# Scores and values of an attention tile placed on TensorE part by part instead of as one chain, and tile 1's loads issued by ScalarE

## The chip, the cores and the metric

The kernel runs on one core of one Trainium2 chip. The metric is the time of one execution on the device in microseconds (us), the lower the better. A core has TensorE (PE, matrix products; its weight loads are listed as PEld), VectorE (DVE), ScalarE (ACT), GpSimd (POOL) and SyncE (SP), which issues most of the DMA transfers. The engines work beside one another and wait for one another through semaphores.

## What is computed

Attention over a window of 128 keys (4 batches, 8 heads, 576 positions, 64 values per head), then a token mixer and two channel MLPs:

```python
scores = q @ k.T / sqrt(64)
scores = where((rel >= 0) & (rel < 128), scores - slope * abs(rel), -1e9)   # rel = query - key
attn = softmax(scores)
x = attn @ v                                   # 4 x 576 x 512
h = relu(x.T @ w_tok1) @ w_tok2                # token mixer
u = x + h.T
x = u + relu(u @ w_ch1) @ w_ch2                # channel MLP, 512 -> 1536 -> 512
out = x + relu(norm(x) * g @ w_ch1b) @ w_ch2b  # second MLP, 512 -> 2048 -> 512
```

## The kernel before

The 2304 positions are cut into 18 tiles of 128. The program first lists operations, each with its engine, a cost, what it reads and what it writes; a planner (`Plan.order`) then plays the engines against these costs, and the order in which it starts the operations is the order in which the instructions are written, engine by engine. On the chip each engine works through its own list in that order. Among the operations that are ready the planner takes the one with the earliest due time, and the due times are worked out from the summed PE costs. The dictionary `pl.chain` makes it place one operation directly behind another; a chained operation must be ready as soon as its forerunner is.

In the attention stage a tile i goes through these steps:

- Scores (line 636): `packed(i, i2)` makes two parts, one for each of two PSUM banks `ps_s` (c = 0, 1). A part is 4 matmuls that use 64 rows of the array each, two at a time on its two halves; a tile that starts a batch (0 and 9) has 128 columns in a matmul, the others 256. The trace lists two instructions for a matmul on f32 here, so a part is 8 rows of the trace and both are 16.
- `softmax(i, c)`: VectorE copies part of the keys over (682), takes scores and bias together with a minimum (688), ScalarE takes the exponentials (697), PE transposes four 128x128 blocks into the one PSUM bank `ps_t` (704), ScalarE (for the first tiles also VectorE) copies them to `pf` (377, 383), and GpSimd masks them (715).
- Values (648): two parts again, 8 matmuls each (4 for a tile that starts a batch), each using 64 columns of the array, two at a time. `normalize` copies them to `ut`, transposes them back (727) and scales them into `u` (393).

In the kernel before, `packed` puts the two scores parts of tile i + 1 and the two values parts of tile i - 1 into one chain on PE. Its first operation is given all that the others read and write (`also`), so that the chain starts only when both banks and both `pf` are there. The costs have 200 ns added at its first and its last operation.

Between these, PE does the token mixer (472 to 474 and 788 to 790: three matmuls of 512 columns for a product, called a triple here), whose weights VectorE, ScalarE and GpSimd convert from 64-bit numbers on the way (441 on ScalarE; 444, 446, 448, 456 on VectorE; one set of these per weight block). After the attention the channel MLPs follow (1177 to 1179 and 1312 to 1314).

The loads: SyncE issues tile 0's keys and queries in halves (568), then tile 1's keys and queries (572 and 369), tile 2's and so on. ScalarE issues the bias (847) and then loads its table (850).

Of the kernel before, what the change touches and what calls it, by code (L numbers as in the profile page):

```python
# [24 lines left out]
P = 128  # L25
DM = H * D
# [5 lines left out]
WINDOW = 128  # L32
RING = 4
WT2_PARTS, FIRST_TILES = 3, 3
CT = 4
CW = CT * P
HW = CW // 2
# [76 lines left out]
class Plan:  # L114
# [22 lines left out]
    def buf(self, pool, shape, dtype, tag, bufs=1):  # L137
        b = Buf(self, pool, shape, dtype, tag, bufs)
        ring = self.rings.setdefault((pool, tag), [])
        if len(ring) >= bufs:  # L140
            b.after = [ring[-bufs]]
        if ring:
            b.behind = ring[-1]
        ring.append(b)
        return b
# [155 lines left out]
    def emit(self):  # L301
        for k in self.order():
            self.ops[k][1](self.taken[k])


def dve(n, fast=False):
    return 150 + n / (1.92 if fast else 0.97)
# [14 lines left out]
def pe(n):  # L322
    return 2.6 + n / 2.4
# [6 lines left out]
def block_kernel(tc, qT, kT, v, wt1, wt2, wa1, wa2, wb1, wb2, g, bias, out):  # L330
    nc = tc.nc
# [4 lines left out]
    def op(cost, emit, reads=(), writes=(), behind=()):  # L336
        return pl.op(cost, (lambda e: emit()) if len(cost) == 1 else emit, reads, writes, behind)
# [30 lines left out]
    def load(dst, get, nbytes, src):  # L368
        op({"DMA": max(nbytes / 360, 500)}, lambda: nc.sync.dma_start(out=get(), in_=src), writes=[dst])
# [124 lines left out]
    src = {"a1": wa1, "a2": wa2, "b1": wb1, "b2": wb2}  # L494
# [55 lines left out]
    bias_sb = buf("att", [P, 4, H, P], BF16, "bias_sb")  # L550
# [5 lines left out]
    keys = buf("att", [P, RING, H // 2, P], F32, "keys")  # L556
# [1 line left out]
    wt2h, wt2l = few()  # L558
    vs, qs = {}, {}

    def load_qk(i):
        r = i % RING
        b = qs[i] = buf("att", [P, H // 2, P], F32, "q", Q_BUFS)
        if i == 0:
            for c in range(2):
                def halves(h=slice(2 * c, 2 * c + 2)):
                    for x, src in ((keys.t[:, 0, h], kT), (b.t[:, h], qT)):
                        nc.sync.dma_start(out=x, in_=src[0].rearrange("p (h t) -> p h t", t=P)[:, h])

                op({"DMA": 1000 if c == 0 else P * DM * 4 / 360}, halves, writes=[b if c else (keys, 0)])  # L570
            return
        op({"DMA": 1000}, lambda: nc.sync.dma_start(out=keys.t[:, r].rearrange("p h t -> p (h t)"), in_=kT[i]),
           writes=[(keys, r)])
        load(b, lambda: b.t.rearrange("p h t -> p (h t)"), P * DM * 4, qT[i])

    def load_v(i):
        b = vs[i] = buf("atb", [P, H, D], F32, "v", 3)
# [25 lines left out]
    def keys_of(i):  # L603

        s = i % RING
        if starts_batch(i):
            return [i], 0, 0, (s, s + 1, 1)
        table = 3 if len(batches_of(i)) > 1 else 2 if len(batches_of(i - 1)) > 1 else 1
        if s == 0:
            return [i, i - 1], 0, table, (0, RING, RING - 1)  # L610
        return [i - 1, i], 1, table, (s - 1, s + 1, 1)
# [6 lines left out]
    def packed(i, i2):  # L618

        parts, ready = [], []
        if i is not None:
            tiles, own, table, (a0, a1, a2) = keys_of(i)
            w = len(tiles) * P
            x = qs[i]
            for c in range(2):
                ps_t[i, c] = buf("psa", [P, 2, 2, 2 * P], F32, "ps_s", 2)  # L630

                def scores(c=c, ps=ps_t[i, c]):
                    for p in range(2):
                        for j in range(2):
                            r = slice(j * D, (j + 1) * D)
                            nc.tensor.matmul(ps.t[:, j, p, :w], x.t[r, 2 * c + p], keys.t[r, a0:a1:a2, 2 * c + p],  # L636
                                             start=True, stop=True)

                parts.append((4 * pe(2 * w), scores, [x] + [(keys, t % RING) for t in tiles], [ps_t[i, c]]))
        if i2 is not None:  # L640
            tiles2 = keys_of(i2)[0]
            na = len(tiles2)
            for c in range(2):
                def values(c=c, pf=pf_t[i2, c]):
                    for p in range(2):
                        for a, kt in enumerate((i2, i2 - 1)[:na]):
                            for j in range(2):
                                nc.tensor.matmul(pv.t[j * D:(j + 1) * D, 2 * c + p], vs[kt].t[:, 4 * c + 2 * p + j],  # L648
                                                 pf.t[:, a, 2 * p + j], start=(a == 0), stop=(a == na - 1))

                parts.append((na * 440, values, [(pf_t[i2, c], a) for a in range(na)] + [vs[kt] for kt in tiles2],
                              [(pv, c)]))

        before = None
        for k, (cost, emit, reads, writes) in enumerate(parts):
            also = parts[k + 1:] if k == 0 else []
            now = op({"PE": cost + (200 if k in (0, len(parts) - 1) else 0)}, emit,
               reads + [x for p in also for x in p[2]], writes + [x for p in also for x in p[3]])
            if before is not None:
                pl.chain[before] = now  # L660
            before = now
        fill(before, 4 if i == 0 else 0)
# [7 lines left out]
    def fill(k, n):  # L670
        if n:
            pl.chain[k] = op({"PE": 0}, lambda: spin(n), [ident], [busy], [k])
# [127 lines left out]
    def attention():  # L800
# [16 lines left out]
        def bias_time(a, b, emit=lambda: None):  # L817
            return op({"DMA": (b - a) * P * P * H * 2 / 360}, emit, [], [(bias_sb, j) for j in range(a, b)])

        def make_bias():  # L820
# [15 lines left out]
            for c in range(2):  # L836
# [7 lines left out]
               one, [(bias_sb, 3)])  # L844

        load_qk(0)
        first = bias_time(0, 1, lambda: nc.scalar.dma_start(out=bias_sb.t[:, 1, 0], in_=bias))
        warm = buf("small", [P, 1], F32, "warm")
        op({"DVE": 60}, lambda: nc.vector.memset(warm.t, 0.0), [], [warm])
        op({"ACT": 1400}, lambda: nc.scalar.activation(out=warm.t, in_=warm.t, func=AF.Exp), [], [warm], [first])  # L850
        load_qk(1)
        make_bias()
        bias_time(1, 2)
        op({"DVE": 0}, lambda: None, [(bias_sb, 0), (bias_sb, 1)], [(bias_sb, 1)])
        load_v(0)
        load_v(1)
        load_qk(2)
        tok_later = []

# [6 lines left out]
        for i in range(-1, NTILE + 1):  # L866
# [15 lines left out]
            for c in range(2):  # L882
# [4 lines left out]
                m, r = divmod(n - WT_START, WT_STEP)  # L887
# [53 lines left out]
    def prep_wide(layer, tiles):  # L941
# [10 lines left out]
        def quadrant(r, c, kk):  # L952
            return turned(layer, [(tiles[CT * c + t], 2 * r + kk) for t in range(CT)])

# [117 lines left out]
    def fast2(s):  # L1072
        layer, c, _, n = steps[s]
        return (layer, c) in FAST2 and n < (NF1, NF2)[layer] // 2 - 1
# [218 lines left out]
    def second(s, w2, hid):  # L1293

        layer, _, tiles, n = steps[s]
        turns = list(enumerate(tiles))
        if s == len(steps) - 1:
            turns = turns[CT:] + turns[:CT]
        for t, i in turns:
            if len(tiles) == 2:  # L1300
                hs = [(*hid[0], j, j * HW + t * P) for j in range(2)]
            else:
                hs = [(*hid[j, t // CT], None, t % CT * P) for j in range(2)]
            if s == len(steps) - 1 and t == turns[-1][0]:
                last_tile(w2, hs, i)
                yield
                continue
            o = buf("pst", [P, DM], F32, "tok", 2)

            def emit(o=o, hs=hs):  # L1310
                for j, ((wh, wl), (hh, hl, _, c)) in enumerate(zip(w2, hs)):
                    nc.tensor.matmul(o.t, hh.t[:, c:c + P], wh.t, start=j == 0, stop=False)  # L1312
                    nc.tensor.matmul(o.t, hh.t[:, c:c + P], wl.t, start=False, stop=False)  # L1313
                    nc.tensor.matmul(o.t, hl.t[:, c:c + P], wh.t, start=False, stop=j == 1)  # L1314

            op({"PE": 6 * pe(DM)}, emit, [x for w in w2 for x in w] + [(x, key) for hh, hl, key, _ in hs for x in (hh, hl)], [o])
            op({"DVE": dve(DM)}, lambda o=o, i=i: nc.vector.tensor_tensor(u[i].t, o.t, u[i].t, ALU.add), [o], [u[i]])  # L1317
            if layer == 1 and n == NF2 // 2 - 1:
                op({"DMA": 728}, lambda i=i: nc.sync.dma_start(out=out[i * P:(i + 1) * P, :], in_=u[i].t), [u[i]])
            yield  # L1320

    def second_fast(s, w2, hid):
# [8 lines left out]
        for g in range(2):  # L1331
            first, other = tiles[2 * g], tiles[CT + 2 * g]
            groups.append([first, other, g, {}])
# [124 lines left out]
    w1, pieces, before = begun(), None, None  # L1458
    load_w(used[0] + W_BUFS)
    for s in range(len(steps) + 1):  # L1460
# [7 lines left out]
        if len(tiles) == 2:  # L1468
            parts, ns = two_blocks(w1, xs, hid), (4, 4)
        else:  # L1470
            parts = seven_products(w1, xs, keep, s == len(steps) - 1, hid, fast2(s))
# [41 lines left out]
        before = s, w2, hid  # L1513
# [41 lines left out]
```

## Time and profile before

| | before |
|---|---|
| time, median of 3 runs | 832.47 us (832.24 to 832.49) |
| the profiled execution, its own time | 832.61 us |
| its span, first to last instruction | 830.9 us |
| PE busy | 820.7 us (99%) |
| DVE busy | 660.7 us (80%) |
| POOL busy | 471.7 us (57%) |
| ACT busy | 429.5 us (52%) |

A span is cut into stretches by the view of windows, which gives the busy time of each engine in each stretch. A busy PE is not a PE at its pace: a matmul's shown duration covers its way through the array, and the next one starts before it ends. What PE needs for a piece of work is therefore read from the starts of successive instructions, not from their durations. Idle time that the views show in front of an instruction is shorter than the time lost there, for the same reason.

### The profile page before, as it was taken

The numbers are of one execution on the slowest core, as the hardware profiler recorded it, in microseconds if no ns is written. First come the engines' busy times: TensorE is split into PE (matmuls) and PEld (weight loads), VectorE is DVE, ScalarE is ACT, GpSimd is POOL, SyncE is SP. The second block draws the span as 40 slices with busy tenths as digits, with TensorE's granted clock in tenths as the row PEclk, the third lists the DMA queues.
The fourth block names the chain that finished last, engine by engine and source line by source line (L and its number), as shares of the span: only waits on it lengthen the run. The fifth ranks groups of instructions, "written<-read, shape, count | busy, mean of one in ns | idle before, by whom it ended". The sixth has DMA issues, their size and how long they took to land.

```text
span 830.9 us, 14390 instructions
## 1 busy us (share of the span) xinstructions
PE 820.7 (99%) x4743; PEld 692.4 (83%) x4743; DVE 660.7 (80%) x1384; ACT 429.5 (52%) x1017; POOL 471.7 (57%) x728
## 2 busy tenths in 40 slices
PE   8999999999999999999999999999999999999998
PEld 6777788888888898888888888888889889999997
DVE  6889777969788979987879868989666767777785
ACT  7888777643344544334368333437456634444440
POOL 4785456746354567534248666857543556666650
PEclk9999999999999999999999999999999999999999
DMA  8578745545668889987862544888977663443302
GB/s 310 170 197 292 240 148 175 167 159 178 219 223 288 294 316 320 350 282 248 284 219 65 183 156 143 289 311 292 348 265 240 228 224 130 133 145 118 102 26 101
DMA packets 80618, 178.19 MB, mean 214 GB/s; under 512 B 9248, under 2 KB 11680, under 8 KB 80544
## 3 DMA queue, kind: packets, MB, share of 16 engines
q1 hardware_dynamic: 79920, 175.94, 62.5%
q0 software_dynamic: 480, 1.31, 0.7%
q8 instruction: 37, 0.61, 0.3%
q14 instruction: 37, 0.30, 0.1%
q10 hardware_dynamic: 144, 0.03, 0.0%
HBM read 137.14 MB, written 38.80 MB: 212 GB/s over the span
## 4 chain that ended last, share of the span: by engine, by line
PE 92%; DVE 4%; ACT 2%; issue 1%; POOL 0%; DVEq 0%; ACTq 0%
PE b L1177 10%; PE tok L1312 10%; PE tok L1314 10%; PE b L1178 10%; PE tok L1313 10%; PE b L1179 10%; PE tok L1349 5%; PE p L1349 4%; PE ps_s L636 3%; PE ps_v L648 3%; PE p L930 2%; PE b L474 2%; PE b L473 2%; PE b L472 2%; PE ps_t L704 1%; ACT pr L697 1%
## 5 line engine op out<-in xcount | busy, mean ns | idle before, releaser
L1317 DVE TENSOR_TENSOR u<-tok,u 128x512 f32<-128x512 f32 x195 | 133.7, 687 | 52.7 <-PE tok L1314 51.3
L1312 PE MATMUL tok<-w2h,hh 128*128 128x512 f32 x390 | 153.3, 393 | 0.0
L1314 PE MATMUL tok<-w2h,hl 128*128 128x512 f32 x390 | 152.1, 390 | 0.1
L1313 PE MATMUL tok<-w2l,hh 128*128 128x512 f32 x390 | 152.2, 390 | 0.0
L1177 PE MATMUL b<-xh,w1h 128*128 128x512 f32 x384 | 150.4, 392 | 0.3 <-DVE b L393 0.3
L1178 PE MATMUL b<-xl,w1h 128*128 128x512 f32 x384 | 149.8, 390 | 0.0
L1179 PE MATMUL b<-xh,w1l 128*128 128x512 f32 x384 | 149.6, 389 | 0.0
L395 POOL TENSOR_TENSOR w1l<-w,w1h 128x256 fp32r<-128x256 f32 (+1 forms) x112 | 79.4, 730 | 111.1 <-ACT w1h L377 97.0
L1008 ACT ACTIVATE hh<-b 128x512 fp32r<-128x512 f32 (+1 forms) x112 | 58.6, 541 | 140.6 <-PE b L1179 99.9
L1314 PEld LDWEIGHTS tok<-w2h,hl 128*128 128x128 f32 x390 | 73.2, 188 | 16.4 <-DVE hl L1010 0.8
L1312 PEld LDWEIGHTS tok<-w2h,hh 128*128 128x128 f32 x390 | 73.3, 188 | 15.0 <-DVE u L1317 0.8
L1010 DVE SCALAR_TENSOR_TENSOR hl<-b,hh 128x512 fp32r<-128x512 f32 (+1 forms) x112 | 67.2, 617 | 23.0 <-ACT hh L1008 22.5
L1313 PEld LDWEIGHTS tok<-w2l,hh 128*128 128x128 f32 x390 | 73.3, 188 | 14.2
L1179 PEld LDWEIGHTS b<-xh,w1l 128*128 128x128 f32 x384 | 72.1, 188 | 15.4
L1177 PEld LDWEIGHTS b<-xh,w1h 128*128 128x128 f32 x384 | 72.2, 188 | 14.5 <-DVE b L393 0.7
L1178 PEld LDWEIGHTS b<-xl,w1h 128*128 128x128 f32 x384 | 72.2, 188 | 13.5
L395 POOL TENSOR_TENSOR w1l<-st,w1h 128x256 fp32r<-128x256 f32 x58 | 44.9, 796 | 48.6 <-ACT w1h L377 42.7
L441 ACT ACTIVATE e<-rh 128x512 bf16<-128x512 bf16 (+2 forms) x62 | 39.7, 640 | 62.5 <-DMA rh<-wb 30.3
L697 ACT ACTIVATE pr<-t,mn 128x128 f32<-128x128 f32 x144 | 55.9, 391 | 10.1 <-DVE mn L688 10.0
L715 POOL TENSOR_SCALAR_AFFINE_SELECT pf<-pf 128x512 f32<-128x512 f32 x64 | 42.2, 660 | 33.3 <-ACT pf L377 26.3
L393 DVE TENSOR_TENSOR b<-b,p 128x512 f32<-128x512 f32 x56 | 38.9, 695 | 20.0 <-PE b L1179 19.5
L395 POOL TENSOR_TENSOR xl<-st,xh 128x256 fp32r<-128x256 f32 x48 | 39.0, 834 | 21.0 <-ACT xh L377 16.6
(215 smaller groups left out, 1931.2 us busy)
## 6 DMA issues: line engine op xcount, KB each, us to landing
w<-d SPq DMA_DIRECT2D x86, 256.0 KB, 4.3
rw<-wb SPq DMA_DIRECT2D x32, 512.0 KB, 5.2
rh<-wb SPq DMA_DIRECT2D x32, 512.0 KB, 5.0
rw<-wa SPq DMA_DIRECT2D x24, 512.0 KB, 4.3
rh<-wa SPq DMA_DIRECT2D x24, 512.0 KB, 4.5
d<-y SPq DMA_DIRECT2D x30, 256.0 KB, 5.4
v<-v SPq DMA_DIRECT2D x18, 256.0 KB, 3.8
keys<-kT SPq DMA_DIRECT2D x17, 256.0 KB, 4.5
```

The lines of the kernel that those rows point to most:

```text
L395: ENGINE[e].tensor_tensor(get()[:, c], ga()[:, c], gb()[:, c], alu)
L697: op({"ACT": 580}, lambda m=m: nc.scalar.activation(out=pr.t[:, m], in_=t.t[:, m], func=AF.Exp, bias=mn.t[:, m:m + 1], scale=-1.0, accum_o ...
L1008: op({"ACT": act(n, True)}, lambda: nc.scalar.activation(out=hh.t[:, c], in_=go(), func=AF.Relu), [o], [(hh, key)])
L1010: mark[0] = op({"DVE": dve(n)}, lambda: nc.vector.scalar_tensor_tensor(out=hl.t[:, c], in0=go(), scalar=0.0, in1=hh.t[:, c].bitcast(F32), ...
L1177: nc.tensor.matmul(g.t, wh.t[:, w], xh.t, start=start and k == 0, stop=False, skip_group_check=True)
L1178: nc.tensor.matmul(g.t, wh.t[:, w], xl.t, start=False, stop=False, skip_group_check=True)
L1179: nc.tensor.matmul(g.t, wl.t[:, w], xh.t, start=False, stop=stop and k == 1, skip_group_check=True)
L1312: nc.tensor.matmul(o.t, hh.t[:, c:c + P], wh.t, start=j == 0, stop=False)
L1313: nc.tensor.matmul(o.t, hh.t[:, c:c + P], wl.t, start=False, stop=False)
L1314: nc.tensor.matmul(o.t, hl.t[:, c:c + P], wh.t, start=False, stop=j == 1)
L1317: op({"DVE": dve(DM)}, lambda o=o, i=i: nc.vector.tensor_tensor(u[i].t, o.t, u[i].t, ALU.add), [o], [u[i]])
L1349: nc.tensor.matmul(o.t[:, p], x()[:, c], y(), start=start and p == 0 and k == 0, stop=stop and p == 1 and k == 2, skip_group_check=True)
```

## The change

- A table `SPLIT` names all 18 tiles. For these the parts are no longer chained, the first no longer takes over what the others read and write, and each part's cost has 100 ns added, instead of 200 at the first and the last.
- Tile 1's keys and queries are issued by ScalarE, right behind the bias and ahead of its table load, and no longer by SyncE. The two operations in the planner stay, with nothing to issue.

```diff
+SPLIT = range(18)
...
-    def load_qk(i):
+    def load_qk(i, ahead=None):
...
-        op({"DMA": 1000}, lambda: nc.sync.dma_start(out=keys.t[:, r].rearrange("p h t -> p (h t)"), in_=kT[i]),
-           writes=[(keys, r)])
-        load(b, lambda: b.t.rearrange("p h t -> p (h t)"), P * DM * 4, qT[i])
+        def start(k, queue=nc.sync):
+            x, src = ((lambda: keys.t[:, r], kT), (lambda: b.t, qT))[k]
+            queue.dma_start(out=x().rearrange("p h t -> p (h t)"), in_=src[i])
+
+        for k, x in enumerate(((keys, r), b)):
+            op({"DMA": (1000, P * DM * 4 / 360)[k]}, (lambda: None) if ahead else (lambda k=k: start(k)), writes=[x])
+        return lambda: [start(k, ahead) for k in range(2)]
...
-            also = parts[k + 1:] if k == 0 else []
-            now = op({"PE": cost + (200 if k in (0, len(parts) - 1) else 0)}, emit,
+            also = parts[k + 1:] if k == 0 and i not in SPLIT else []
+            now = op({"PE": cost + (100 if i in SPLIT else 200 if k in (0, len(parts) - 1) else 0)}, emit,
                reads + [x for p in also for x in p[2]], writes + [x for p in also for x in p[3]])
-            if before is not None:
+            if before is not None and i not in SPLIT:
                 pl.chain[before] = now
...
-        first = bias_time(0, 1, lambda: nc.scalar.dma_start(out=bias_sb.t[:, 1, 0], in_=bias))
+        first = bias_time(0, 1, lambda: (nc.scalar.dma_start(out=bias_sb.t[:, 1, 0], in_=bias), second()))
...
-        load_qk(1)
+        second = load_qk(1, nc.scalar)
```

The last chains have no scores in them (i is None), and stay as they were. In the changed kernel the lines stand 5 further down (scores 641, values 653, transposes 709 and 732; the lines ahead of `load_qk` 1 further: the triples 473 to 475, the weight conversion 445, 447, 449 and 457).

On PE, early in the attention stage (tiles 5 to 7). Before:

```order
L636 MATMUL ps_s<-keys,q 128x256 x8
L648 MATMUL ps_v<-pf,v 64x128 x16
L704 MATMUL ps_t<-ident,pr 128x128 x4
L727 MATMUL ps_v<-ident,ut 128x128 x4
L472 MATMUL tok<-xh,wt1h_406 128x512
L473 MATMUL tok<-xl,wt1h_406 128x512
L474 MATMUL tok<-xh,wt1l_423 128x512
L704 MATMUL ps_t<-ident,pr 128x128 x4
L472 MATMUL tok<-xh,wt1h_406 128x512
```

Now:

```order
L641 MATMUL ps_s<-keys,q 128x256 x4
L709 MATMUL ps_t<-ident,pr 128x128 x4
L653 MATMUL ps_v<-pf,v 64x128 x16
L641 MATMUL ps_s<-keys,q 128x256 x4
L709 MATMUL ps_t<-ident,pr 128x128 x4
L732 MATMUL ps_v<-ident,ut 128x128 x4
L641 MATMUL ps_s<-keys,q 128x256 x4
L709 MATMUL ps_t<-ident,pr 128x128 x4
L653 MATMUL ps_v<-pf,v 64x128 x16
```

The two scores parts of a tile stand apart, each alone between transposes and values, and the triples that stood between the transposes are gone from this place and come later.

On VectorE, at the same tiles (`t` is the scores with their bias, `mn` their minimum, `s`, `m` and `y` a weight block on its way). Before:

```order
L732 RECIPROCAL rc<-rc 128x8
L393 TENSOR_TENSOR u<-ps_v,rc 128x512
L444 TENSOR_SCALAR s<-e 128x128
L446 SCALAR_TENSOR_TENSOR s<-e,s 128x128
L456 SCALAR_TENSOR_TENSOR y<-m,s 128x256
L448 TENSOR_SCALAR m<-rw 128x256
L682 COPY_PREDICATED ps_s<-after,ps_s 128x4x128 x2
L688 ISA t,mn<-ps_s,bias_sb 128x128
```

Now:

```order
L693 ISA t,mn<-ps_s,bias_sb 128x128
L693 ISA mn 128x1
L445 TENSOR_SCALAR s<-e 128x96
L449 TENSOR_SCALAR m<-rw 128x192
L447 SCALAR_TENSOR_TENSOR s<-e,s 128x96
L687 COPY_PREDICATED ps_s<-after,ps_s 128x4x128
L457 SCALAR_TENSOR_TENSOR y<-m,s 128x192
L693 ISA t,mn<-ps_s,bias_sb 128x128
```

Before, the scores of both banks come together, with one weight block for a tile; now they come bank by bank, and a weight block stands between the banks as well.

On PE, late in the attention stage (the scores of tile 16). Before:

```order
L704 MATMUL ps_t<-ident,pr 128x128 x4
L636 MATMUL ps_s<-keys,q 128x256 x8
L648 MATMUL ps_v<-pf,v 64x128 x16
L472 MATMUL tok<-xh,wt1h_406 128x512
L473 MATMUL tok<-xl,wt1h_406 128x512
```

Now:

```order
L795 MATMUL tok<-hh,fewl 128x512
L641 MATMUL ps_s<-keys,q 128x256 x4
L709 MATMUL ps_t<-ident,pr 128x128 x4
L653 MATMUL ps_v<-pf,v 64x128 x16
L641 MATMUL ps_s<-keys,q 128x256 x4
L709 MATMUL ps_t<-ident,pr 128x128 x4
```

Where PE went from its whole array to scores, to values and back once, it now goes to scores, back, to values, to scores and back.

## Rows read from the trace of the kernel before

**Rows 1.** Windows: busy us (x instructions) per engine, granted clock, DMA share, GB/s.

```profile
6.03:50.70 44.67, 42.28 (x404) 33.12 (x401) 37.80 (x177) 36.62 (x145) 27.20 (x49) 1.00 0.71 234
...
48.47:88.05 39.58, 37.16 (x360) 29.31 (x358) 34.68 (x152) 33.53 (x127) 25.98 (x51) 1.00 0.83 260
88.05:156.56 68.51, 68.51 (x548) 56.52 (x548) 54.91 (x164) 47.23 (x142) 40.93 (x60) 1.00 0.58 192
156.56:830.90 674.34, 670.01 (x3446) 571.83 (x3444) 534.51 (x905) 310.61 (x607) 375.08 (x558) 1.00 0.63 213
```

**Rows 2.** Timeline of PE around one chain: start us, us, engine, line, operation.

```profile
96.37 2.00 PE L636 MATMUL ps_s<-keys,q 64*128 64x256 f32 x16
98.29 1.97 PE L648 MATMUL ps_v<-pf,v 128*64 128x128 f32 x32
100.19 0.66 PE L704 MATMUL ps_t<-ident,pr 128*128 128x128 f32 x4
...
102.08 0.60 PE L727 MATMUL ps_v<-ident,ut 128*128 128x128 f32 x4
102.51 0.60 PE L704 MATMUL ps_t<-ident,pr 128*128 128x128 f32 x4
```

**Rows 3.** Timeline of PE in four narrow windows inside that chain.

```profile
96.90 0.60 PE L636 MATMUL ps_s<-keys,q 64*128 64x256 f32 x4
...
97.77 0.60 PE L636 MATMUL ps_s<-keys,q 64*128 64x256 f32 x4
...
98.78 0.50 PE L648 MATMUL ps_v<-pf,v 128*64 128x128 f32 x6
...
99.77 0.50 PE L648 MATMUL ps_v<-pf,v 128*64 128x128 f32 x6
```

**Rows 4.** Timeline of PE around values that stand alone, late in the stage.

```profile
135.48 0.40 PE L473 MATMUL tok<-xl,wt1h 128*128 128x512 f32 x1
135.71 0.40 PE L474 MATMUL tok<-xh,wt1l 128*128 128x512 f32 x1
136.04 1.97 PE L648 MATMUL ps_v<-pf,v 128*64 128x128 f32 x32
137.93 0.50 PE L472 MATMUL tok<-xh,wt1h 128*128 128x512 f32 x1
138.28 0.40 PE L473 MATMUL tok<-xl,wt1h 128*128 128x512 f32 x1
```

**Rows 5.** Timeline of PE: tile 1's scores, with the idle time ahead of them.

```profile
7.59 2.00 PE L636 MATMUL ps_s<-keys,q 64*128 64x256 f32 x16 [0.61 <-DVE mn L688]
```

**Rows 6.** PE's groups by form from 48.47 to 88.05 us: busy, mean ns | idle, releaser.

```profile
L648 PE MATMUL ps_v<-pf,v 128*64 128x128 f32 x176 | 10.9, 276 | 0.0
L704 PE MATMUL ps_t<-ident,pr 128*128 128x128 f32 x48 | 8.7, 289 | 1.7 <-ACT pf L377 1.5
L636 PE MATMUL ps_s<-keys,q 64*128 64x256 f32 x66 | 8.4, 389 | 0.0
L727 PE MATMUL ps_v<-ident,ut 128*128 128x128 f32 x24 | 3.7, 276 | 0.3 <-ACT ut L377 0.3
L788 PE MATMUL tok<-hh,fewh 128*128 128x512 f32 x8 | 3.6, 448 | 0.0
...
L473 PE MATMUL tok<-xl,wt1h 128*128 128x512 f32 x2 | 0.9, 445 | 0.4 <-POOL xl L395 0.4
```

**Rows 7.** VectorE's groups from the start to 50.7 us, by line.

```profile
L688 DVE CUSTOM_DVE_ANT_0 t<-ps_s,bias_sb 128x128 f32<-128x128 f32 x64 | 14.5, 285 | 1.8 <-PE ps_s L636 1.8
...
L446 DVE SCALAR_TENSOR_TENSOR s<-e,s 128x128 int32<-128x128 int32 x5 | 2.9, 570 | 0.1
L456 DVE SCALAR_TENSOR_TENSOR y<-m,s 128x256 f32<-128x256 uint32 x5 | 2.4, 484 | 0.1
L448 DVE TENSOR_SCALAR m<-rw 128x256 uint32<-128x256 uint32 (+1 forms) x6 | 2.4, 397 | 0.6 <-DMA rw<-wt 0.5
L444 DVE TENSOR_SCALAR s<-e 128x128 int32<-128x128 int32 x5 | 1.6, 314 | 0.0
```

## The prediction, written before the result was known

> **What bounds the kernel now.** I read the windows first. From 88.05 us to the end of the stage at 156.56, where the first channel matmul starts, PE has no idle time, and behind it 670.0 of 674.3 us are busy [rows 1]. So PE sets the end, and whatever the attention stage loses or gains up to 156.56 us is passed on to the end nearly one to one. Between 48.47 and 88.05 PE shows 2.4 us of idle time, and earlier 2.4 us of the 44.67 us from 6.03 to 50.70 [rows 1]. The granted clock is 1.00 (2.4 GHz) in all of these.
>
> Then I read what PE's work costs, from starts. A triple's matmul comes 0.23 us after the one before it (135.48 to 135.71) [rows 4]. Transposes come 0.43 / 4 = 0.108 us apart [rows 2]. A scores part, 8 listed instructions, takes 97.77 - 96.90 = 0.87 us [rows 3]. 18 listed instructions of values take 0.99 us, so the 32 of a tile take 1.76 [rows 3].
>
> Last, what it costs to change between whole array, scores and values. In the chain, scores last 98.29 - 96.37 = 1.92 us for 1.74 of work, values 100.19 - 98.29 = 1.90 for 1.76 [rows 2]: 0.18 and 0.14 over. Values that stand alone start 0.33 us after a triple's matmul instead of 0.23, last 1.89 for 1.76, and the matmul behind them gives way to the next after 0.35 instead of 0.23 [rows 4]: 0.10 + 0.13 + 0.12 = 0.35 for two changes. With entry, the two overheads and an exit of about half of 0.12 (a transpose follows mostly), a chain pays some 0.5 for three. I take **0.165 us a change**, with 0.15 and 0.18 as ends.
>
> **The change part by part.**
>
> *Changes on PE.* Counted in the order of the two programs, PE changes between the three kinds 56 times before and 106 times now: 33 groups of scores for 18, 25 of values for 18. That is 50 x 0.165 = 8.3 us of PE time added. The matmuls are the same. Ten of the changes go from values straight to scores, which the trace of before never does; I give them the same 0.165, between nothing (1.65 us less in the sum) and 0.18. The Trainium skill, TensorEngine Tiling (Array Packing), section Key Properties, says that a change of the tiling mode drains TensorE, though a change of tile within a mode doesn't. The rows above agree for three of the four kinds of change; by that rule the ten pay as well and the sum below stands, without it the sum is 1.65 us less.
>
> *What can be won.* Only PE's waits. First I cut the stage where the scores of tiles 0 to 7 are through, at 48.47 us before.
>
> Up to there, PE's list holds 38.6 us of work before (counts of the order times the prices above) and 20 changes, 3.3 us: 41.9 in all. Now it holds 36.2 us and 35 changes, 5.8: 42.0 in all. Six of eight triples have gone to later (6 x 0.69 = 4.1 us), one tile's values (1.76) have come forward. So to the same place PE has as much to do, with less of the work done. The question is whether it gets there sooner: call the shift d. VectorE decides. From 6.03 to 50.70 us, the start of tile 0's statistics to the end of the 64 of tiles 0 to 7, it is busy 37.8 of 44.67 us [rows 1, 7]. In the new order it has 10 weight blocks instead of 7 ahead of that place, the three more being 192 wide: one costs 0.57 + 0.48 + 0.40 + 0.31 = 1.76 us at 256 [rows 7], so about 1.3, and three 4.0; one more copy from PSUM makes some 0.5. That is 42.3 of 44.67 us. So d can't be under -2.4, and if VectorE kept all its waits of 6.9 us it would be +4.5. Its waits get shorter, because scores reach it bank by bank; I take **d = 0**, at which its share would be 95%.
>
> From there to 156.56: the 2.4 us of work that was put off come in, +2.4. There are 71 changes for 36, 35 x 0.165 = +5.8. Against it stand the waits that are left. From 48.47 to 88.05 PE's work is 176 x 0.055 + 66 x 0.109 + 72 x 0.108 + 30 x 0.23 (ten triples) = 31.5 us [rows 6], the scores of tile 9, which starts a batch, are 0.9, and 18 changes 3.0. Of 39.58 us [rows 1], 4.2 are left: waits. Shown are 2.4, and they are for `pf` from ScalarE (1.7, ahead of transposes), `ut` (0.3) and `xl` from GpSimd (0.4) [rows 6]. Now no two groups of transposes stand directly behind one another any more, and scores stand between values and their transposes, so I count the first two as filled and leave 0.4 for `xl`: -3.8. From 88.05 us on there is nothing to fill [rows 1], and the 18 changes more that I count there are paid in full.
>
> *Tile 1's loads.* Before, tile 1's scores start at 7.59 us when VectorE has freed the bank, after 0.61 us of idle time [rows 5], and not when a load lands. So the loads gain nothing there by themselves. Earlier loads cover an earlier start of the first part, which needs only the first bank now; the gain is at most that 0.61. The loss, if the new loads slow those of tile 0, I put at no more than the same 0.61, as an estimate. I take 0. Work that ScalarE has to do behind the two issues waits for VectorE's first results anyway, which is when 6.03 us has come; it is not costed.
>
> **The sum:** 0 (d) + 2.4 + 5.8 - 3.8 = +4.4 us. The profiled execution took 832.61 us, of which 1.7 lie outside the span and stay: 837.0. It lies 0.14 above the median, so I predict **836.9 us**.
>
> Bounds: with 0.15 a change, all of the waits filled, and d = -2.4, it is 2.4 + 5.25 - 4.2 - 2.4 = +1.0, 833.5. With 0.18, half of the waits left and d = +1.5 (a third of the way to VectorE's keeping its waits) it is 2.4 + 6.3 - 2.1 + 1.5 = +8.1, 840.6.
>
> **The rivals.**
>
> *VectorE keeps its waits (slower than I say).* Without triples in between, PE runs into the banks at tiles 3 to 8: of a tile it has 4.8 us of work and 5 changes, 5.6 us, where VectorE with two weight blocks has more. For it: rows 7 show VectorE waiting for scores before, and each part now waits for it. Against it: banks come one at a time. With d = +3 the sum is +7.4: 839.9.
>
> *The waits go and cancel the changes (no difference).* All 4.2 us filled, d = -1.5, changes from values to scores free: 2.4 + 5.8 - 1.65 - 4.2 - 1.5 = +0.85, 833.3. For it: PE now reaches each place later than the planner thinks, since a part alone costs 0.35 of changes and the planner counts 0.1, so other engines are ahead of it. Against it: it needs VectorE busy at nearly 100% for 40 us.
>
> *The start runs at PE's pace (faster).* Up to 48.47 us PE waits 48.47 - 41.9 = 6.6 us, 1.1 of them ahead of its first matmul. If scores that come singly took five of these away, d = -5, all of the later waits were filled and the ten changes free, the sum is 2.4 + 5.8 - 1.65 - 4.2 - 5 = -2.65: 829.8. It decides at d = -4.0 (with those other two), where 0.2% are reached. Against it: VectorE's sum allows only -2.4, so it needs the three weight blocks to cost next to nothing, and cheaper statistics too.
>
> That the change does nothing can be left out: the order shows the parts apart.
>
> **How the numbers follow.** A measurement can tell about 0.2%, 1.7 us, from no change. The forecast, from 834.1 to 838.9, has 0.58; VectorE's waits, above that, 0.15; no difference, 830.8 to 834.1, 0.19; faster 0.08. Slower is the first two: 0.73. The likeliest case gives 836.9. The range goes from 833.4, the low bound, to 840.6, the high one; below it I leave the faster case and a part of the case of no difference, above it little.
>
> **What would show it.** Right: the first channel matmul (1182 in the new lines) starts at about 161 us instead of 156.56; the pairs of changes show as 0.3 us and more over the work of every part that stands alone, values to scores among them; PE has no idle time in the last 70 us of the stage; VectorE is 95% busy up to the 64th statistic, which comes at about 50.7 us. Wrong: if that statistic comes before 48 us, d was mis-sized; if it comes at 53 or later, the first rival holds; if the stage ends before 158 us with the parts as they stand, the changes cost less than 0.165. If stage and end disagree by more than 1 us, something behind 156.56 moved, which I have put at nothing since PE's list there differs in a few places only and its waits were short.

## The result, and the profile after

The changed kernel takes 839.17 us (median of 6 runs, 837.86 to 841.84), the kernel before 832.48 (6 runs, 832.24 to 833.92). The ratio is 1.0081, interval 1.0071 to 1.0092: 6.7 us slower. The forecast was 836.9, 4.4 us slower, with 840.6 as the upper bound; the sign was right and the size 2.3 us short. The profiled execution is the longest of the six: 841.84 us, a span of 840.1 against 830.9, so 9.2 us more. Rows of this execution are measured against that 9.2, not against the 6.7.

First the windows that answer [rows 1], cut where the 16th scores part (tiles 0 to 7) ends, where the waits end, and at the first channel matmul. Columns: busy us (x instructions) of PE, PEld, DVE, ACT, POOL, granted clock, DMA share, GB/s.

```profile
6.03:48.32 42.29, 40.78 (x383) 30.71 (x383) 37.08 (x174) 34.46 (x141) 25.96 (x49) 1.00 0.86 248
48.32:58.20 9.88, 6.70 (x35) 4.48 (x35) 6.86 (x38) 5.44 (x19) 5.32 (x12) 0.65 1.01 254
58.20:166.49 108.29, 108.29 (x862) 83.05 (x859) 77.61 (x265) 76.01 (x247) 60.87 (x98) 1.00 0.56 183
166.49:840.10 673.61, 669.56 (x3446) 571.77 (x3444) 538.89 (x911) 310.28 (x607) 373.28 (x545) 1.00 0.63 214
```

Up to 48.32 us nothing is lost: the kernel before is at the same place at 48.47. Behind 58.20 PE has no idle time left up to the first channel matmul, which starts at 166.49 instead of 156.56, 9.9 us later; 0.7 of that comes back behind it. Between the two lies a stretch that the kernel before does not have: 3.2 of 9.88 us shown idle, a mean clock of 0.65, and the DMA engines full.

The whole attention stage in one row each, from 6.03 us to the first channel matmul: the kernel before, and then after.

```profile
6.03:156.56 150.53, 145.72 (x1274) 116.89 (x1271) 125.29 (x475) 116.14 (x407) 92.05 (x154) 1.00 0.68 223
```

```profile
6.03:166.49 160.46, 155.77 (x1274) 118.25 (x1275) 121.55 (x475) 115.91 (x406) 92.15 (x156) 0.98 0.67 205
```

With the same number of matmuls, PE is busy 10.05 us more, and idle 160.46 - 155.77 = 4.69 us against 4.81. (The time lost between unlike matmuls counts as busy here: the rows below show later starts and no idle time.) So none of the waits were saved in sum, and the loss is in busy time.

The timeline of PE around parts that stand alone, against [rows 2 to 4] (start us, us, engine, line, operation):

```profile
20.18 1.97 PE L653 MATMUL ps_v<-pf,v 128*64 128x128 f32 x32
22.07 1.13 PE L641 MATMUL ps_s<-keys,q 64*128 64x256 f32 x8
23.14 0.66 PE L732 MATMUL ps_v<-ident,ut 128*128 128x128 f32 x4
23.63 0.60 PE L709 MATMUL ps_t<-ident,pr 128*128 128x128 f32 x4
...
31.27 0.40 PE L475 MATMUL tok<-xh,wt1l 128*128 128x512 f32 x1
31.60 1.13 PE L641 MATMUL ps_s<-keys,q 64*128 64x256 f32 x8
32.66 0.66 PE L709 MATMUL ps_t<-ident,pr 128*128 128x128 f32 x4
33.25 0.44 PE L653 MATMUL ps_v<-pf,v 128*64 128x128 f32 x4
```

A scores part alone lasts 32.66 - 31.60 = 1.06 us for 0.87 of work [rows 3]; the triple's matmul ahead of it gives way after 0.33 instead of 0.23, and the four transposes behind it after 0.59 instead of 0.43: 0.19 + 0.10 + 0.16 = 0.45 for three changes. Values followed straight by scores, the pair that the trace of before never shows, last 22.07 - 20.18 = 1.89 for 1.76, and the scores then 1.07: these changes cost like the others.

At the start, the answer to [rows 5] (in brackets: idle time ahead, and what ended it):

```profile
6.50 1.23 PE L641 MATMUL ps_s<-keys,q 64*128 64x128 f32 x8 [0.64 <-DMA q<-qT]
...
8.70 1.23 PE L641 MATMUL ps_s<-keys,q 64*128 64x256 f32 x4
```

Tile 0's second part now waits 0.64 us for its queries, and tile 1's scores start at 8.70 instead of 7.59.

Now the stretch from 48 us on, the timeline of all engines:

```profile
48.32 0.66 PE L709 MATMUL ps_t<-ident,pr 128*128 128x128 f32 x4
...
49.37 0.37 ACT L442 ACTIVATE e<-rh 128x192 bf16<-128x192 bf16 x1 [1.78 <-DMA rh<-wt]
...
49.77 0.21 DVE L445 TENSOR_SCALAR s<-e 128x96 int32<-128x96 int32 x1 [1.72 <-ACT e L442]
...
50.16 0.58 ACT L378 ACTIVATE ut<-ps_v 128x512 f32<-128x512 f32 x1
...
50.80 1.00 PE L732 MATMUL ps_v<-ident,ut 128*128 128x128 f32 x4 [1.82 <-ACT ut L378]
...
51.55 0.32 DVE L449 TENSOR_SCALAR m<-rw 128x192 uint32<-128x192 uint32 x1 [1.57 <-DMA rw<-wt]
...
53.16 2.08 PE L641 MATMUL ps_s<-keys,q 64*128 64x256 f32 x8 [1.36 <-DVE mn L693]
55.17 1.11 PE L709 MATMUL ps_t<-ident,pr 128*128 128x128 f32 x4
```

ScalarE converts a weight block and stands at 442 until the block's rows `rh` have landed. Behind it in its queue is the copy `ut`, for which PE waits, and behind that copy the next `pf`. VectorE stands as well, for that conversion and then for `rw`; with it the statistics are late, so the bank for the next scores part is not free. All three engines wait for two loads. SyncE's timeline has their issues:

```profile
43.66 0.80 SPq L430 DMA_DIRECT2D rh<-wt  x1
...
45.57 1.60 SPq L430 DMA_DIRECT2D rw<-wt  x2
```

From 43.66 to about 49.3 are 5.6 us. The view of DMA issues from 40 to 50 us shows what made them long: median us from issue to landing, and the queues' shares; after first, then before.

```profile
q1 hardware_dynamic: 1181, 1.86, 64.8%
q0 software_dynamic: 240, 0.66, 38.1%
...
rw<-wt SPq DMA_DIRECT2D x3, 192.0 KB, 5.8
...
rh<-wt SPq DMA_DIRECT2D x2, 192.0 KB, 6.5
```

```profile
q1 hardware_dynamic: 893, 1.44, 49.7%
...
rw<-wt SPq DMA_DIRECT2D x2, 192.0 KB, 3.0
...
rh<-wt SPq DMA_DIRECT2D x1, 192.0 KB, 3.1
```

The same loads land in 3.0 us before and in about 6 now. The weight blocks come sooner in the new order, and their loads and GpSimd's own transfers of finished weights (q0, none in this window before) now meet the tiles' loads. That this meeting is what slows the loads is read from these views; no run changed it alone.

PE is slow there even where it is busy:

```profile
51.50:58.00 6.50, 5.14 (x25) 3.26 (x24) 6.45 (x36) 3.37 (x15) 2.48 (x6) 0.52 0.96 215
```

Windows of 0.5 us put the granted clock at 0.50 (1.2 GHz) from about 51.0 to 57.8 us, 6.8 us, and at 1.00 (2.4 GHz) around it; before, it is 1.00 throughout the stage. What PE did ahead of the fall is in the row at 50.80: it had been idle for 1.82 us. The Trainium skill, TensorE: Matmul & The Clock Gate, Part 1: The HAM clock gate, says that the gate is set by how busy PE has been. This trace agrees in so far as the fall follows the hole, and the clock falls nowhere else in the stage.

VectorE's groups up to 55.75 us, by line and by form, against [rows 7]:

```profile
L693 DVE CUSTOM_DVE_ANT_0 t<-ps_s,bias_sb 128x128 f32<-128x128 f32 x64 | 15.1, 279 | 2.9 <-PE ps_s L641 2.8
...
L445 DVE TENSOR_SCALAR s<-e 128x96 int32<-128x96 int32 x5 | 1.4, 278 | 2.1 <-ACT e L442 2.1
L449 DVE TENSOR_SCALAR m<-rw 128x192 uint32<-128x192 uint32 x4 | 1.2, 293 | 1.6 <-DMA rw<-wt 1.6
```

The 64th statistic, which started at 50.67 us before, starts at 55.48.

### The profile page after: what moved, and what is told of

The parts are those of the page before. It is cut to its first block, busy times and chain, and to the rows that moved or that the text cites. A ratio compares the mean times of both kernels' runs of the same rounds, so it can differ in the third digit from the quotient of the medians.

```text
span 840.1 us, 14369 instructions
## 1 busy us (share of the span) xinstructions
PE 830.1 (99%) x4743; PEld 693.1 (83%) x4743; DVE 661.3 (79%) x1390; ACT 428.9 (51%) x1016; POOL 470.1 (56%) x717
## 4 chain that ended last, share of the span: by engine, by line
PE 94%; DVE 3%; DMA 1%; ACT 0%; issue 0%; POOL 0%; SPq 0%; ACTq 0%
PE tok L1319 11%; PE tok L1317 11%; PE b L1182 11%; PE tok L1318 10%; PE b L1183 10%; PE b L1184 10%; PE tok L1354 5%; PE p L1354 4%; PE ps_s L641 3%; PE ps_v L653 3%; PE p L935 2%; PE ps_t L709 2%; PE b L475 2%; PE b L474 2%; PE b L473 2%; PE tok L473 1%
## 5 line engine op out<-in xcount | busy, mean ns | idle before, releaser
L396 POOL TENSOR_TENSOR w1l<-st,w1h 128x256 fp32r<-128x256 f32 x70 | 55.9, 820 | 53.9 <-ACT w1h L378 45.9
L396 POOL TENSOR_TENSOR st<-w 128x128 f32<-128x128 f32 x72 | 39.5, 572 | 23.4 <-PE tok L1319 5.6
```

The costliest lines, as they stand in the source:

```text
L396: ENGINE[e].tensor_tensor(get()[:, c], ga()[:, c], gb()[:, c], alu)
```

## Experiments

Two theories on the time that the forecast did not have. **C**: it is all changes on PE, at about 0.17 us each, with little waiting saved against them. **W**: weight blocks that come sooner crowd the DMA queues, a load is late, PE runs dry and its clock falls. A third, **L**, is tile 1's loads: that they slow those of tile 0.

**The loads alone.** All tiles chained as before, tile 1's loads issued by ScalarE.

```diff
-SPLIT = range(18)
+SPLIT = ()
```

> Tile 1's loads issued by ScalarE, scores and values chained as before; the order of all else is that of before. In the changed kernel the second scores part of tile 0 starts at 6.50 us after 0.64 us of waiting for its queries, and tile 1's scores at 8.70 instead of 7.59. Theory L (the earlier loads of tile 1 slow those of tile 0): the same wait shows here, and 0.5 to 1.0 us come on top, 833.0 to 833.5. Theory C (the changes between whole array, scores and values carry the loss) and theory W (the weight blocks brought forward carry it): nothing to measure, 832.5 within 0.4.

Measured: 833.24 us (10 runs) against 832.62 for the kernel before; ratio 1.0009, 1.0000 to 1.0018. PE's waits, in the view of waits (us in total, times, longest), have a new one:

```profile
PE ps_s L641 <- DMA q<-qT: 0.8, 1, 0.8
```

The first channel matmul starts at 156.67, 0.1 later than before. The loads gain nothing and cost some 0.6 us, with an interval from 0 to 1.5; theory L's number came out. The Trainium skill, DMA: Bandwidth & Descriptors, section Issuing engines are not separate DMA queues, says that transfers from several engines interleave on the same 16 DMA engines, and that issuing from more of them saves no more than the time of issuing. This run agrees: with tile 1's loads issued beside them, tile 0's two query loads of 128 KB land in 3.7 us (median) instead of 2.5. In the four kernels with tile 1's loads on ScalarE it is 3.6 to 3.9 us, in the nine others 2.4 to 2.8.

**The placing alone.** All tiles singly, tile 1's loads by SyncE as before.

```diff
-        first = bias_time(0, 1, lambda: (nc.scalar.dma_start(out=bias_sb.t[:, 1, 0], in_=bias), second()))
+        first = bias_time(0, 1, lambda: (nc.scalar.dma_start(out=bias_sb.t[:, 1, 0], in_=bias),))
...
-        second = load_qk(1, nc.scalar)
+        load_qk(1)
```

> Parts placed singly, all loads issued by SyncE. Theory L: 0.5 to 1.0 us less than the changed kernel's 839.2, some 838.4. Theories C and W: as the changed kernel, 837.9 to 840, since the loads do nothing to the order.

Measured: 839.58 us (4 runs), ratio 1.0077 (1.0060 to 1.0094). The whole loss is in the placing: without ScalarE's loads nothing is gained, where theory L expected 0.5 to 1.0 us. Its timeline has the same hole, some 3 us earlier, with the load of `rw` ahead of it:

```profile
48.09 0.93 DVE L449 TENSOR_SCALAR m<-rw 128x192 uint32<-128x192 uint32 x1 [1.66 <-DMA rw<-wt]
49.71 0.38 ACT L442 ACTIVATE e<-w 128x192 bf16<-128x192 bf16 x1 [2.12 <-DVE s L447]
...
50.31 2.08 PE L641 MATMUL ps_s<-keys,q 64*128 64x256 f32 x8 [2.50 <-DVE mn L693]
```

The clock is at 0.50 from 49.8 to 56.6 us there, by windows of 0.5 us: it falls inside the hole.

**The changed kernel with the weight blocks held back.** The first ScalarE step of each block (442) waits for the exponentials of the tile behind which the kernel before has it. 104 changes, 6 triples instead of 2 ahead of the 16th scores part.

```diff
+        first_of.append(len(pl.ops))
         op({"ACT": act(n)}, lambda: nc.scalar.activation(
...
+    HOLD_AT = (1, 2, 3, 4, 5, 6, 7, 7, 8, 9, 9)
...
+        for k, at in zip(first_of, HOLD_AT):
+            pl.ops[k][3].add(last_exp[at, 1])
         pl.emit()
```

> The changed kernel, with the first step of each of the 11 weight blocks of the token mixer held back in the planner to the tile at which it stood before; 104 changes instead of 106, 6 triples instead of 2 ahead of the 16th scores part (before: 8). Theory W: the hole of PE at 48 to 58 us and the half clock behind it go, and with them most of the loss: 834 to 835, clock 1.00 in all runs. Theory C: the hole goes, but 48 more changes at 0.175 us are left against 4 to 6 us of filled waits: 836 to 838.

Measured: 837.78 us (837.43 to 838.02, 4 runs), ratio 1.0059 (1.0044 to 1.0074). The stage, up to its first channel matmul:

```profile
6.03:162.45 156.42, 152.98 (x1275) 115.53 (x1275) 119.23 (x476) 114.64 (x404) 91.63 (x153) 1.00 0.66 213
```

No wait of PE is above 0.9 us, and the clock stays at 1.00. (ScalarE stands once, for 1.15 us, for `rh` at 62.56 us, and no hole follows: a late load does not always reach PE.) PE is idle for 3.44 us, 1.37 less than before, and busy 7.26 more: 0.151 for each of 48 changes. So even without the hole the new order saves 1.4 us of waiting, and not the 3.8 of the forecast. Against the changed kernel's profiled execution 2.79 us of busy time are gone, 0.3 of them two changes: some 2.5 us are the clock. So W is real, but it is worth 1.4 us in the medians (839.17 - 837.78, with intervals of the ratio that just touch) and 4 in the profiled execution; C has the larger part, 5.2 us.

**Only the late tiles singly.** Tiles 9 to 17, 80 changes, loads by ScalarE.

```diff
-SPLIT = range(18)
+SPLIT = range(9, 18)
```

> Only tiles 9 to 17 placed singly (loads by ScalarE as in the changed kernel); the weight blocks of the mixer stand as before, and there are 80 changes, 24 more than before. Theory C: 24 x 0.175 = 4.2 us less 1 to 2 us of waits that are filled: 834.7 to 835.7. Theory W: nothing is brought forward, so 832.5 within 0.7.

Measured: 835.33 us (6 runs), ratio 1.0035 (1.0023 to 1.0047). The clock is 1.00 in the profiled execution. Busy time up to the first channel matmul (159.87) is 149.79 us, 4.07 more than before for 24 changes: 0.170 each. As C has it. Such prices are rough: the kernel with the loads alone, which has no change more, is busy 146.20 us up to that matmul, 0.48 more than before, and against it the 24 changes cost 0.150 each.

**Changes without any other order.** In the order of the kernel before, one more transpose in each of the 18 chains that have scores, into a bank that the scores then overwrite: between its two scores parts (two more changes each), or ahead of the first (next to none). The difference of the two is the price of 36 changes alone.

```diff
                 def scores(c=c, ps=ps_t[i, c]):
+                    if c == 1:
+                        nc.tensor.transpose(ps.t[:, 0, 0, :P], ident.t, ident.t)
```

> The kernel before, its order kept, with one more transpose of a constant 128x128 block in each of the 18 chains, placed between its two scores parts and overwritten by the second: 18 x 0.108 = 1.9 us of work and 36 more changes between whole array and scores. Theory C, that a change costs 0.165 to 0.175 us wherever it stands: 36 x 0.17 = 6.1 us, so 832.5 + 8.0 = 840.5, less 1 to 3 us that fall into waits there are before 88 us: 837.5 to 839.5. Theory N (a change costs little of itself, and the rows read it wrongly): 832.5 + 1 to 2 us, 833.5 to 834.5. In the trace the scores parts on either side of the transpose then show whether each pays 0.1 at its end and 0.1 at its start.

```diff
                 def scores(c=c, ps=ps_t[i, c]):
+                    if c == 0:
+                        nc.tensor.transpose(ps.t[:, 0, 0, :P], ident.t, ident.t)
```

> The same with the transpose ahead of the first scores part: the same 1.9 us of work, and no change more. Both theories: 832.5 + 1 to 2 us, 833.5 to 834.5. What e5 takes over this run is what 36 changes cost.

Measured: 838.94 us (ratio 1.0073, 1.0058 to 1.0088) and 833.73 (1.0015, 1.0005 to 1.0024). The difference is 5.2 us, 0.145 a change. The timeline of the first shows one of them:

```profile
92.18 1.13 PE L638 MATMUL ps_s<-keys,q 64*128 64x256 f32 x8
93.24 0.33 PE L634 MATMUL ps_s<-ident 128*128 128x128 f32 x1
93.50 1.13 PE L638 MATMUL ps_s<-keys,q 64*128 64x256 f32 x8
```

The part lasts 1.06 us for 0.87 and the transpose 0.26 for 0.108: 0.34 for two changes. Side by side a change costs 0.17; in the whole stage 0.14 to 0.15 come out, and why it is less there is not settled: PE's shown idle time in the stage differs by 0.2 us only (4.42 and 4.62). C stands by itself, without a hole and at full clock.

**Fewer changes: the two scores parts in one chain, the two values parts in another, placed apart.** 69 changes, loads by SyncE.

```diff
+            mine = "s" if i is not None and k < 2 else "v"
...
-            if before is not None and i not in SPLIT:
+            if mine == kind:
                 pl.chain[before] = now
```

> All loads by SyncE; the two scores parts of a tile stay one chain, the two values parts stay another, but the two chains are placed apart, each with 100 ns added to a part's cost: 69 changes instead of 56, 6 triples ahead of the 16th scores part, the weight blocks nearly as before. Theory C: 13 x 0.175 = 2.3 us more of changes against up to 5 us of waits filled: 830.5 to 833. Theory W: the blocks stay, so nothing holds PE up and the waits are filled: 829 to 831.

Measured: 835.73 us (834.22 to 838.60, 6 runs), ratio 1.0038 (1.0024 to 1.0053). Both theories were wrong on it. Its trace has the signature again, later: a load that ScalarE stands for, and then ten microseconds with idle time on PE and a lower mean clock.

```profile
69.41 0.38 ACT L442 ACTIVATE e<-rh 128x192 bf16<-128x192 bf16 x1 [1.88 <-DMA rh<-wt]
```

```profile
70.00:80.00 10.00, 7.68 (x55) 5.61 (x52) 7.01 (x32) 8.46 (x31) 4.64 (x11) 0.83 0.91 311
```

**Only tiles 0 to 3 singly.** 63 changes, 7 more than before, loads by SyncE.

```diff
-SPLIT = range(18)
+SPLIT = range(4)
```

> All loads by SyncE; only tiles 0 to 3 placed singly, where PE waits most: 63 changes instead of 56, 6 triples instead of 8 ahead of the 16th scores part. Theory C: 7 x 0.175 = 1.2 us of changes against 1 to 2 us of waits: 831.5 to 833. Theory W: the weight blocks come later here (25 exponentials ahead of the first, before 16), nothing is brought forward: 830.5 to 832.

Measured: 838.83 us (836.79 to 839.99, 4 runs), ratio 1.0077 (1.0060 to 1.0094): as slow as the full change, with 7 changes for 50. Both theories as I had put them were wrong. Its windows from 60 to 70 us, and the timeline of all engines there:

```profile
60.00:64.00 4.00, 1.11 (x14) 0.70 (x10) 2.83 (x22) 1.66 (x7) 3.45 (x9) 1.00 1.16 265
64.00:70.00 6.00, 3.41 (x13) 2.04 (x15) 3.45 (x11) 4.75 (x20) 3.01 (x5) 0.69 1.03 228
```

```profile
63.41 0.37 ACT L442 ACTIVATE e<-rh 128x192 bf16<-128x192 bf16 x1 [2.35 <-DMA rh<-wt]
...
64.70 0.66 PE L732 MATMUL ps_v<-ident,ut 128*128 128x128 f32 x4 [3.60 <-ACT ut L378]
```

PE works 4.5 of 10 us, and then at half clock. By 170 us it has issued 1311 matmuls where the kernel before has 1338. Of the 6.2 us, 7 changes are 1.2 at most, so the hole and the clock behind it can cost some 5. And W does not need blocks that come sooner than before: here they come later, but closer together. ScalarE starts the 6th to 9th block between 52.35 and 63.41 us, and before between 47.81 and 62.20; the 9th is the one that waits.

**The same two with the blocks spaced.** The tile behind which each block starts is set by hand, so that the 8th to 10th come 8 exponentials, one tile, apart (the expectation has it as 8 tiles' exponentials, for the 8th to 11th). For the kernel of tiles 0 to 3 (the one of pairs has the same lines):

```diff
+    HOLD_AT = (1, 2, 3, 4, 5, 6, 7, 8, 9, 10, 10)
...
+        for k, at in zip(first_of, HOLD_AT):
+            pl.ops[k][3].add(last_exp[at, 1])
```

> The kernel of e8 (tiles 0 to 3 placed singly, loads by SyncE, 63 changes), with the first ScalarE step of the weight blocks held so that the 8th to 11th block come 8 tiles' exponentials apart: the row block that was asked for 5.6 us after its load was issued in e8 is asked for later. Theory H (the single row buffer, reloaded in about 5.8 us, makes ScalarE stand, TensorE runs dry and its clock halves; placing singly only moves the blocks into that place): no wait of e for rh over 0.5 us, no stretch at half clock, and 832.5 + 7 changes x 0.17 = 833.7 us less what falls into waits, 832 to 835. Theory R (placing the first tiles singly costs its 4 to 6 us by itself, whatever the blocks do): 836.5 to 839 as e8.

Measured: 835.74 us (6 runs), ratio 1.0035 (1.0020 to 1.0050); 3.1 us off the kernel without the spacing, and still 3.3 above before. Neither number was met: it lies between H's 832 to 835 and R's 836.5 to 839. ScalarE no longer waits for `rh`, but VectorE now waits for `rw`, and PE for what is behind it:

```profile
65.33 0.50 DVE L450 TENSOR_SCALAR m<-rw 128x192 uint32<-128x192 uint32 x1 [1.88 <-DMA rw<-wt]
...
67.15 0.80 PE L797 MATMUL tok<-hh,fewh 128*128 128x512 f32 x1 [2.45 <-DVE hl L774]
```

SyncE issued the two loads of `rw` from 59.06 us on; from 56 to 68 us their median from issue to landing is 6.2 us, with GpSimd's queue at 59.0%. The clock fell again (mean 0.996). The spacing moved the late load; it did not take it away.

> The kernel of e7 (pairs of scores and of values placed apart, loads by SyncE, 69 changes) with the same holding of the weight blocks. Theory H: e7's wait of 1.9 us for the row block, its hole and its half clock go; 832.5 + 13 changes x 0.17 = 834.7 us less up to 4 us of waits that filling takes away: 831 to 835, and the granted clock 1.0 to 80 us. Theory R: 835.7 as e7, since the changes and the new order cost it.

Measured: 836.12 us (4 runs), ratio 1.0041 (1.0025 to 1.0057), against 835.73 without the spacing. The windows of the profiled execution:

```profile
60.00:70.00 10.00, 9.67 (x99) 7.39 (x101) 8.15 (x43) 9.98 (x44) 8.71 (x17) 1.00 0.91 247
70.00:80.00 10.00, 8.72 (x78) 6.21 (x74) 7.51 (x33) 8.47 (x33) 5.75 (x11) 1.00 0.73 243
```

The hole and the half clock are gone in this execution (two of the four runs have a mean clock of 0.998), and the time is not better: it is theory R's 835.7 that came out. The profiled execution (835.42 us) is 2.9 above the kernel before. Its first channel matmul comes at 159.46 us, also 2.9 later, with 1.3 us more of busy time and 1.6 more of idle: PE is idle for 6.4 us up to there, against 4.8 before. The 13 changes would be 2.0 to 2.2 at 0.15 to 0.17, more than the busy time shows, so that split is rough; but more waiting is about half of the loss. That the new order takes nothing from the waits, even without a late load, is what the expected 831 to 835 had missed.

> Control: the kernel before with the same holding of the weight blocks and nothing else (56 changes as before). Theory H: the kernel before has no wait for a row block, so the holding gives nothing; it moves two triples' worth of work behind the 28th scores part: 832 to 833.5 us. If it is faster or slower by more than 1 us, e9 and e10 have to be read against it and not against the kernel before.

Measured: 832.38 us (10 runs), ratio 0.9998 (0.9989 to 1.0008). The spacing by itself does nothing to the kernel before, so the two runs above can be read against it. It also shows how rough busy time is: with the same 56 changes PE is busy 0.97 us more up to the first channel matmul (146.69 us). No version that was run is measurably faster than the kernel before.

## Why the prediction was right, and where it was short

Its steps, in its order:

- **PE sets the end; a loss up to the first channel matmul is passed on.** Right: +9.9 at that matmul, +9.2 in the span.
- **50 more changes at 0.165, +8.3 us.** The mechanism was right, values to scores included. The size is about 0.15: (10.05 - 2.5) / 50 = 0.151 in the changed kernel, 0.151 in the held one, 0.150 to 0.170 with the late tiles alone, 0.145 in the pair of transposes, which alone is a difference of times and not of busy time. That is the low end that was given, some 0.8 us less than the term.
- **d = 0 up to the 16th scores part.** Right: 48.32 us against 48.47. VectorE's work was well sized too, 41.5 us for 42.3; but it was to be done in 44.67 us, at 95%, and took until 55.74, at 83%.
- **Waits of 4.2 us after that, 0.4 of them left.** This is the step that failed. The waits it spoke of, for `pf`, `ut` and `xl` between 48 and 88 us, are gone as it said: PE shows no idle time from 58.20 us on. A new one of 3.2 us stands ahead of them, which the forecast did not have, so that PE's idle time in the stage is 4.69 us where it was 4.81. Nor is the hole all that was missed: in the held kernel, which has none, 1.37 us of idle time are saved and not 3.8. It had counted the three more weight blocks as VectorE's work alone, and not their loads and GpSimd's transfers, although it shows the DMA share ([rows 1], 0.83 from 48.47 to 88.05) and VectorE's waits for `rw` ([rows 7], 0.5 us).
- **The clock at 1.00 throughout.** An assumption that was not written into the sum. It fell for 6.8 us, worth some 2.5 in the profiled execution. As an estimate from the row at 51.50, 5.14 us of busy time at half speed, of which half would do at most, give 2.6.
- **Tile 1's loads, 0 within 0.61.** Their own run gives +0.6, at the edge of what can be told; the row at 6.50 us shows where. The placing without them is no faster (839.58 us).

With the price of the pair of transposes the sum for the profiled execution is 0.145 x 50 - 0.1 + 2.5 = +9.65 us at the first channel matmul, against 9.93 by the windows. (With 0.151, which was taken from this execution itself, it comes out of necessity.) Against the forecast's +4.4 these are 5.5 us: 3.7 of waits not saved and 2.5 of the clock, less some 0.8 for cheaper changes. The medians differ by less, 6.7, in part because the clock does not fall as long in each run: the six runs have mean granted clocks between 0.996 (841.84 and 840.36 us) and 1.000 (837.86), though not in strict order (838.61 us at 0.997, 839.74 at 0.999). That the time lies under the upper bound of 840.6 is partly luck: that bound was made of dearer changes, half of the waits and d = +1.5, and of these only the waits came, with a fall of the clock that stood in no term.

The rival that VectorE keeps its waits set a sign, the 64th statistic at 53 us or later, and a time, 839.9. The sign came true (55.48) and the time is nearer than the forecast's. Its mechanism did not: it had PE run into the banks at tiles 3 to 8 and d at +3, and d is -0.15. VectorE waited behind that, for a load. The sign was too coarse to tell the two apart; a sign at the 16th scores part would have.

What stays open: how much of the late landing is due to GpSimd's transfers and how much to the weight and tile loads that meet them. All come sooner or closer together at once, and a kernel that moves one of them alone was not tried. The views of DMA issues from 58 to 70 us give a hint. There the kernel before moves 2.51 MB by the hardware queue and 0.66 by GpSimd's, and 192 KB land in 3.6 and 4.5 us (`rw`, `rh`); the kernel of pairs moves 2.27 and 1.00 MB, and they land in 6.3 and 5.5. So less by the one and more by the other goes with later landing.

## What to carry to other kernels

A chain that keeps matmuls of one array shape together saves a fixed time at each change of shape; breaking it up pays only if it removes more waiting than changes times that time, and here 50 changes cost 7.5 us where only 4.8 us of idle time were there to win. Where a planner sets the order, a looser placing on one engine moves the loads and conversions of quite other work; look at what now lands in the same microseconds, and whether an engine with something urgent in its queue waits there for a load. A hole on PE can cost more than its length, since the clock may fall behind it.

## What the runs showed of the hardware

- A load of 192 KB landed in 3.0 us with the hardware queue alone at work (49.7% of 16 engines' time), and in 5.8 to 6.5 us with that queue at 64.8% and GpSimd's at 38.1%, both by the view of DMA issues from 40 to 50 us. GpSimd's queue beside it is not enough: in the held kernel, with 41.7% and 20.0% from 36 to 52 us, it landed in 2.7 to 3.3.
- The clock fell to 1.2 GHz in the middle of a busy program and came back 6.8 us later: in the changed kernel after 1.82 us of shown idle time, with the placing alone inside a hole of 2.50. In the kernel with tiles 0 to 3 singly the mean clock was 0.995 in the profiled run (836.79 us) and 0.992 in the longest (839.99).
- Two loads of 256 KB issued by ScalarE beside SyncE's first ones let SyncE's query loads of 128 KB land in 3.6 to 3.9 us, in four kernels, where they took 2.4 to 2.8 in nine others. PE waited 0.6 to 1.3 us for them.
- One more 128x128 transpose between two scores parts, which is a change from 64 rows to the whole array and back, cost 0.145 us for each of the two changes by the difference of two runs (5.2 us for 36).
